# A retention and two feed-forward layers: the beginning and the first block join the played order

## The chip, the cores and the metric

The kernel runs on one core of one Trainium2 chip. The metric is the time of one execution on the device in microseconds (us). The engines are TensorE (PE, matmuls), VectorE (DVE), ScalarE (ACT), GpSimd (POOL) and SyncE (SP, which here issues nearly all transfers). Each engine takes its own instructions strictly in order.

## The reference

Three stages in float32, for 4 x 576 = 2304 tokens, 8 heads of 64, model width 512, inner width 2048:

```python
scores = q @ k.T / sqrt(64)                     # per batch and head
ret    = scores * where(i >= j, gamma_h ** (i - j), 0)
x      = (ret @ v), heads side by side          # 2304 x 512
h = x @ moe_w_in;   g = maximum(0.01 * h, h);  x = g @ moe_w_out
h = x @ moe2_w_in;  g = h * cos(h);            out = g @ moe2_w_out
```

## The kernel before

The tokens are cut into 18 chunks of 128 for the attention and into five blocks for the first layer (`TB`, line 27). The attention runs as a recurrence: per chunk `scores` (64 x 64 products of k and q), `masks` (DVE multiplies by the causal mask), `values` and `growth` (products with v, and the growth of the state), `states` (DVE adds the growth to the running state), `reads` (PE adds the state's share), and `take` (ACT scales the result into `xr`). `scale_q` and `scale_v` multiply a chunk's q and v by tables beforehand.

The first layer needs its operands as a high and a low half of 32 bits each, and the weights arrive as 64-bit words, two 32-bit words to a value. There are 16 weight tiles f (128 of the 2048 inner columns each; the tile holds its part of w_in and of w_out). One tile is converted by ACT (absolute value `conv_a` line 445, scaling of the low word line 446, cast to the high half line 473) and DVE (clamp 451, shift 453, sign 457, addition 464, and the low half, by subtraction, 476). Blocks of x are split likewise (`split_x`, ACT 492, DVE 493). `h_mm` (H, line 505) is x times a tile's w_in, `o_mm` (O, line 519) is g times its w_out: 12 matmuls each. Between them ACT applies the leaky ReLU and casts (530, 535), DVE makes g's low half (540). O trails H by two tiles (`LAG`): H0, H1, H2, O0, H3, O1 and so on. While a block runs, the chunks of the next are computed between its steps ("visits").

The order of work is written in two ways. The beginning (chunks 0 to 3) and block 0 are written out by hand in lines 1324 to 1434: transfers, attention and conversions in the order in which each engine is to take them. From block 1 on, `rest` gives every piece of work to a `Plan` (line 85) with an engine, an estimated duration, what it needs, and a due time; `play` (line 98) walks through it as a list scheduler would and writes the instructions in the order in which they began there. `dma` and `dve` add such tasks. The played part also converts the second layer's weights (lines 971 to 1043) beside blocks 1 to 3, and stores them for the second layer, which multiplies by Strassen-like sums.

SP waits for the landing of the eighth transfer before each new one, beside the buffers a transfer needs. A raw weight tile lies in the room of a later weight tile (`ROOM`, line 548), which it must leave before that tile is written.

Of the kernel before, what the change touches and what calls it, by code (L numbers as in the profile page):

```python
# [19 lines left out]
P = 128  # L20
# [6 lines left out]
TB = (512, 512, 512, 384, 384)  # L27
T0 = (0, 512, 1024, 1536, 1920)
# [24 lines left out]
G = 3  # L53
# [21 lines left out]

LATE, DRAIN = 12, 6
# [71 lines left out]
def retention_ffn_ffn(  # L148
# [43 lines left out]
    zero = xp.tile([P, 2 * T], F32, tag="x", name="zero")[:, :P]  # L192
# [23 lines left out]
    def scale_q(i):  # L216
        q = ch_t[i][:, 0]

        eng = nc.gpsimd if n_busy <= i < n_busy + 2 else nc.vector
        eng.tensor_tensor(out=q, in0=q, in1=itab_sb, op=ALU.mult)  # L220

    def scale_v(i):
        c = i % CYCLE * H
        if i in (1, 2) or n_first <= i < n_busy:
# [6 lines left out]
        eng = nc.gpsimd if 0 < i < n_busy + 2 else nc.vector  # L231
        eng.tensor_tensor(out=v3, in0=v3, in1=t3, op=ALU.mult)
# [86 lines left out]
    def growth(i):  # L319
# [16 lines left out]
        if i > n_first:  # L336
            last_of["rows"] = rows_done(got)
# [17 lines left out]
    def reads(i, part):  # L355

        v, ch = banks_of(i)[1], ch_t[i]
        behind = [last_of.pop("rows")] if part else []
# [19 lines left out]
        if not part:  # L378
            last_of["part", i] = last_of["rows"] = rows_done(last_of["pe", i])

    def both_reads(i):
        reads(i, 0)
        reads(i, 1)
# [11 lines left out]
    def take(i, ps=range(NP)):  # L395
# [39 lines left out]
    def words(g):
        r = raw_t[g].bitcast(U32).rearrange("p (x t) -> p x t", t=2)
        return r[:, :, 0], r[:, :, 1]

    def conv_a(g):
        lo, hi = words(g)  # L440
        n = lo.shape[1]
        whole = multi.tile([P, 2 * DM], F32, tag="t", name="t32")
        t = whole[:, :n]
        t_t[g], rawp_t[g] = t, whole
        nc.scalar.activation(t, hi.bitcast(F32), AF.Abs)
        nc.scalar.mul(lo.bitcast(I32), lo, 2.0**-29)

    def conv_b(g, between=lambda: None):
        lo, hi = words(g)
        t = t_t[g]  # L450
        nc.vector.tensor_scalar(t, t, W_LO, W_HI, op0=ALU.max, op1=ALU.min)
        u = t.bitcast(U32)
        nc.vector.tensor_scalar(  # L453
            u, u, 3, 0x3FFFFFF8, op0=ALU.logical_shift_left, op1=ALU.bitwise_and
        )
        between()
        nc.vector.scalar_tensor_tensor(  # L457
            out=u, in0=hi, scalar=0xC0000000, in1=u, op0=ALU.bitwise_and, op1=ALU.bitwise_or
        )

    def conv_c(g):
        lo, _ = words(g)
        i = t_t[g].bitcast(I32)
        nc.vector.tensor_tensor(out=i, in0=i, in1=lo.bitcast(I32), op=ALU.add)  # L464
        raw_t.pop(g)

    def w_part(g, half):
        l, f, s = g
        wt = w_t[l, f]
        return wt[:, half] if s is None else wt[:, half, s * DM : (s + 1) * DM]  # L470

    def conv_d(g):
        nc.scalar.copy(w_part(g, 0), t_t[g])

    def conv_e(g, eng):
        eng.tensor_tensor(
            out=w_part(g, 1), in0=t_t.pop(g), in1=w_part(g, 0).bitcast(F32), op=ALU.subtract
        )

    def new_w(l, f):  # L480
        w_t[l, f] = w_tile(f, [P, 2, 2 * DM], F32R, f"w{f}")


    x_t, h_t, g_t, graw = {}, {}, {}, {}

    def split_x(lj):
        n = TB[lj]
        for k in range(KK):
            x = xp.tile([P, 2, T], F32R, tag="x", name="x_sb")
            x_t[lj, k] = x  # L490
            raw = xr.pop((lj, k))[:, :n]
            nc.scalar.copy(x[:, 0, :n], raw)
            nc.vector.tensor_tensor(  # L493
                out=x[:, 1, :n], in0=raw, in1=x[:, 0, :n].bitcast(F32), op=ALU.subtract
            )
# [31 lines left out]
    def leaky(lj, f):  # L527
        hp = h_t.pop((lj, f))
        g = gp.tile([P, T], F32, tag="graw", name="graw", bufs=G)[:, : TB[lj]]
        nc.scalar.activation(g, hp, AF.Prelu, alpha=0.01)  # L530
        graw[lj, f] = g

    def g_high(lj, f):
        g_t[lj, f] = gp.tile([P, 2, T], F32R, tag="g", name="g")
        nc.scalar.copy(g_t[lj, f][:, 0, : TB[lj]], graw[lj, f])

    def g_low(lj, f):
        n = TB[lj]
# [54 lines left out]
    def rest():  # L593
# [53 lines left out]
        for s in range(NF, len(steps) + LAG):  # L647
# [841 lines left out]
```

## Time and profile before

| | us |
|---|---|
| three runs | 856.03, 856.01, 853.37 (median 856.01) |
| profiled execution | 853.42 |
| its span, first to last instruction | 851.3 |
| PE busy | 829.3 |
| DVE busy | 601.5 |
| ACT busy | 518.4 |
| POOL busy | 8.5 |

The mean granted clock of PE is 0.986 of full speed. The part of the execution outside the span is 2.1 us. Busy shares are means over stages: block 0 ends near 140 us, the first layer near 471, and the rest is the second layer.

### The profile page before, as it was taken

The numbers are of one execution on the slowest core, as the hardware profiler recorded it, in microseconds if no ns is written. First come the engines' busy times: TensorE is split into PE (matmuls) and PEld (weight loads), VectorE is DVE, ScalarE is ACT, GpSimd is POOL, SyncE is SP. The second block draws the span as 40 slices with busy tenths as digits, with TensorE's granted clock in tenths as the row PEclk, the third lists the DMA queues.
The fourth block names the chain that finished last, engine by engine and source line by source line (L and its number), as shares of the span: only waits on it lengthen the run. The fifth ranks groups of instructions, "written<-read, shape, count | busy, mean of one in ns | idle before, by whom it ended". The sixth has DMA issues, their size and how long they took to land.

```text
span 851.3 us, 16302 instructions
## 1 busy us (share of the span) xinstructions
PE 829.3 (97%) x6288; PEld 771.0 (91%) x6288; DVE 601.5 (71%) x1183; ACT 518.4 (61%) x1112; POOL 8.5 (1%) x9
## 2 busy tenths in 40 slices
PE   6699999999999999999999999999999999999998
PEld 6478888888888888999999999999999999999998
DVE  4799985776876757667511587889877876866762
ACT  4688864554655545555422688767678755677650
POOL 0000020000000000000000000000000000000000
PEclk7799999999999999999999999999999999999999
DMA  9925512656657866853790798798988697665312
GB/s 358 418 83 202 192 67 85 217 194 211 211 191 251 247 213 197 260 191 135 262 406 2 252 311 272 265 374 322 349 284 287 216 405 272 208 225 186 137 49 75
DMA packets 91949, 193.30 MB, mean 227 GB/s; under 512 B 7648, under 2 KB 55264, under 8 KB 81632
## 3 DMA queue, kind: packets, MB, share of 16 engines
q1 hardware_dynamic: 91728, 191.92, 64.2%
q8 instruction: 49, 0.80, 0.4%
q10 hardware_dynamic: 144, 0.35, 0.1%
q14 instruction: 28, 0.23, 0.1%
HBM read 143.22 MB, written 49.02 MB: 226 GB/s over the span
## 4 chain that ended last, share of the span: by engine, by line
PE 90%; DMA 4%; issue 3%; DVE 2%; ACT 1%; SPq 0%; POOLq 0%; DVEq 0%
PE psum L1239 23%; PE psum L519 22%; PE psum L505 21%; PE psum L1111 19%; DMA raw<-in_w 2%; PE psum L366 1%; PE psum L305 1%; PE psum L328 1%; PE psum L268 1%; DMA wa<-wa 1%; DMA ws<-ws 1%; DVE t L464 0%; DVE st L351 0%; DVE t L457 0%; DVE t L453 0%
## 5 line engine op out<-in xcount | busy, mean ns | idle before, releaser
L1239 PE MATMUL psum<-g,wo 128*128 128x384 f32 x1152 | 222.3, 334 | 0.0
L505 PE MATMUL psum<-x_sb,w 128*128 128x512 f32 (+1 forms) x960 | 214.2, 373 | 4.2 <-DVE x_sb L493 2.5
L519 PE MATMUL psum<-g,w 128*128 128x512 f32 (+1 forms) x960 | 212.0, 370 | 0.0
L505 PEld LDWEIGHTS psum<-x_sb,w 128*128 128x128 f32 x960 | 177.5, 190 | 29.7 <-DVE x_sb L493 2.7
L1239 PEld LDWEIGHTS psum<-g,wo 128*128 128x128 f32 x1152 | 201.7, 188 | 0.0
L519 PEld LDWEIGHTS psum<-g,w 128*128 128x128 f32 x960 | 174.3, 188 | 23.7
L1111 PE MATMUL psum<-x,ws 128*128 128x384 f32 x576 | 114.5, 335 | 1.3 <-ACT psum L1212 1.3
L1111 PEld LDWEIGHTS psum<-x,ws 128*128 128x128 f32 x576 | 100.9, 188 | 2.3 <-ACT psum L1212 1.9
L797 DVE TENSOR_TENSOR g<-graw,g 128x512 fp32r<-128x512 f32 (+1 forms) x64 | 39.9, 623 | 69.3 <-ACT g L794 69.0
L1111 PE MATMUL psum<-x,wa 128*128 128x384 f32 x432 | 86.1, 334 | 0.0
L1111 PEld LDWEIGHTS psum<-x,wa 128*128 128x128 f32 x432 | 75.9, 188 | 0.0
L1166 DVE SCALAR_TENSOR_TENSOR h<-r,h 128x384 f32<-128x384 f32 x96 | 52.9, 554 | 24.0 <-ACT r L1163 23.7
L794 ACT CAST g<-graw 128x512 fp32r<-128x512 f32 (+1 forms) x64 | 36.3, 568 | 48.8 <-PE psum L519 47.0
L790 ACT ACTIVATE graw<-psum 128x512 f32<-128x512 f32 (+1 forms) x64 | 34.7, 542 | 48.2 <-PE psum L505 47.5
L1162 ACT ACTIVATE r<-r 128x384 f32<-128x384 f32 x96 | 50.4, 525 | 21.2 <-DVE r L1155 20.7
L1150 DVE SCALAR_TENSOR_TENSOR r<-n,h 128x384 f32<-128x384 int32 x96 | 53.0, 552 | 11.9 <-ACT n L1147 11.5
L1176 DVE TENSOR_TENSOR g<-h,g 128x384 fp32r<-128x384 f32 x96 | 52.7, 553 | 10.9 <-ACT g L1173 10.3
L1147 ACT ACTIVATE n<-h 128x384 int32<-128x384 f32 x96 | 49.3, 519 | 8.4 <-DVE h L1139 8.0
L1155 DVE SCALAR_TENSOR_TENSOR r<-n,r 128x384 f32<-128x384 int32 x96 | 53.2, 554 | 1.6
L1173 ACT CAST g<-h 128x384 fp32r<-128x384 f32 x96 | 48.6, 509 | 7.6 <-DVE h L1166 7.3
L1163 ACT ACTIVATE r<-r 128x384 f32<-128x384 f32 x96 | 50.5, 526 | 2.0
L1258 DVE SCALAR_TENSOR_TENSOR acc<-psum,acc 128x384 f32<-128x384 f32 x48 | 26.7, 557 | 16.4 <-PE psum L1239 15.3
(81 smaller groups left out, 794.8 us busy)
## 6 DMA issues: line engine op xcount, KB each, us to landing
ws<-ws SPq DMA_DIRECT2D x24, 1024.0 KB, 7.1
wo<-wo SPq DMA_DIRECT2D x24, 1024.0 KB, 6.0
wa<-wa SPq DMA_DIRECT2D x24, 768.0 KB, 6.1
ch<-in_qkv SPq DMA_DIRECT2D x17, 1024.0 KB, 7.7
mraw<-in_w SPq DMA_DIRECT2D x64, 256.0 KB, 3.6
x<-xq SPq DMA_DIRECT2D x21, 768.0 KB, 9.6
raw<-in_w SPq DMA_DIRECT2D x15, 1024.0 KB, 9.1
xq<-m SPq DMA_DIRECT2D x84, 128.0 KB, 5.1
```

Source lines behind the costliest of these rows:

```text
L505: nc.tensor.matmul(hp, wt[:, i, cols], x_t[lj, k][:, j, :n], start=(k == 0 and a == 0), stop=(k == KK - 1 and a == 2),)
L519: nc.tensor.matmul(psum[:, BANK_O + m, :n], wt[:, i, cols], gt[:, j, :n], start=(f == 0 and a == 0), stop=(f == NF - 1 and a == 2),)
L1111: nc.tensor.matmul(bank[BANKS[m]], a[:, hl, i, j * P : (j + 1) * P], x[:, j, v, :], start=m in (1, 5) and j == 0 and n == 0, stop=j == 1 a ...
L1147: t = add("ACT", 515, lambda: nc.scalar.activation(n_ap(), hb.ap, AF.Copy, scale=INV_2PI), [t], due, 0, nb.old)
L1150: nc.vector.scalar_tensor_tensor(out=r_ap(), in0=n_ap(), scalar=-C1, in1=hb.ap, op0=ALU.mult, op1=ALU.add)
L1155: nc.vector.scalar_tensor_tensor(out=r_ap(), in0=n_ap(), scalar=-C2, in1=r_ap(), op0=ALU.mult, op1=ALU.add)
L1162: t = add("ACT", 515, lambda: nc.scalar.activation(r_ap(), r_ap(), AF.Sin, scale=0.5), [t], due)
L1163: t = add("ACT", 515, lambda: nc.scalar.activation(r_ap(), r_ap(), AF.Square), [t], due)
L1166: nc.vector.scalar_tensor_tensor(out=hb.ap, in0=r_ap(), scalar=0.5, in1=hb.ap, op0=ALU.subtract, op1=ALU.mult)
L1173: t = add("ACT", 515, lambda: nc.scalar.copy(gb.ap[:, 0], hb.ap), [t], due, 0, gb.old)
L1176: nc.vector.tensor_tensor(out=gb.ap[:, 1], in0=hb.ap, in1=gb.ap[:, 0].bitcast(F32), op=ALU.subtract)
L1239: nc.tensor.matmul(bank[m], wt[:, i, hl, m * P : (m + 1) * P], gt[:, v, :], start=h == 0 and z == 0 and x == 0, stop=h == 1 and z == 1 and ...
```

## The change

The hand-written beginning and block 0 go; both become tasks of the same plan. The helpers `load_raw`, `conv_a` to `conv_e`, `split_x`, `leaky`, `g_high`, `g_low` and the hand-written list are deleted; `first_chunk`, `first_weights` and `beginning` take their place. Plan time starts at `BEGIN` = 27 us for the first H. The instructions on a tile are the same, but tile 0, like tile 15 before, is converted in two halves of 512 columns (the w_in half, then the w_out half), and all tiles use two fixed buffers, f even the first, f odd the second. The widths of blocks 1 to 4 change order, so block 0 now has three chunks to visit for block 1 beside chunk 3's half visit, not four. POOL keeps only the scaling of chunk 3's v; the scalings of chunks 8 and 9, which it had, go to DVE.

```diff
-TB = (512, 512, 512, 384, 384)
-T0 = (0, 512, 1024, 1536, 1920)
+TB = (512, 384, 384, 512, 512)
+T0 = (0, 512, 896, 1280, 1792)
...
+BEGIN, IN_HALVES = 27, (0, NF - 1)
...
+    def v_by(i):
+        return {0: "DVE", 1: "ACT", 2: "ACT", 3: "POOL"}.get(i, "ACT" if i < n_busy else "DVE")
...
-        at, now = {}, 0.0
+        at, now = {}, BEGIN
...
+        def chunk(i, due):
+
+            old = () if i < n_first else read_of[i - n_first if i < n_first + 2 else i - 2]
+            t = dma(2650, lambda: load_chunk(i), old, due - 14, (), 4000 if i < n_first else 2500)
+            a = dve(DVE[512], lambda: scale_q(i), [t], due - 4)
...
+        def first_chunk(i):
+            due = i / 10 - SOON
+            if i:
+                chunk(i, 14 + i)
+            c = [add("PE", 900, lambda: scores(i), scaled[i], due)]
+            m = [add("DVE", 700, lambda: masks(i), c, due)]
+            v = [add("PE", 900, lambda: values(i), m, due)]
+            g = [add("PE", 900, lambda: growth(i), v, due)]
+            old = read_of.get(i - 1, ())
+            s_ = [add("DVE", 850, lambda: states(i), [*g, *read_of.get(("st", i - 1), ())], due, 0, old)]
+            read_of["st", i] = s_
+            a = add("PE", 500, lambda: reads(i, 0), s_, due)
+            mark = add("POOL", 60, lambda: None, [a], due)
+            read_of[i] = [add("PE", 500, lambda: reads(i, 1), [mark], due)]
+            taking(i, read_of[i], due)
...
+        def first_weights(f):
+
+            due = at["H", 0, f] - 9
+            halves = [slice(0, DM), slice(DM, 2 * DM)] if f in IN_HALVES else [slice(0, 2 * DM)]
+            tb, t32 = ((t0, t32_0), (t1, t32_1))[f % 2]
+            uses = [Use(b) for b in tb]
+            old_t = uses[0].old + uses[1].old
...
+            for n, h in enumerate(halves):
...
+                got = [loads[n]] if len(loads) > 1 else loads
+                d_ = due + n * 5
+                ab = add("ACT", 630 if one_ else 1140, lambda g=step: g("a"), got, d_, 0, old_t)
+                lo_ = add("ACT", 630 if one_ else 1140, lambda g=step: g("m"), got, d_)
+                t = dve(421 if one_ else 690, lambda g=step: g("c"), [ab], d_)
+                t = dve(421 if one_ else 690, lambda g=step: g("s"), [t], d_)
+                t = dve(690 if one_ else 1225, lambda g=step: g("o"), [t], d_)
+                t = dve(690 if one_ else 1225, lambda g=step: g("+"), [t, lo_], d_)
+                done_ += [t]
+                hi_ = add("ACT", 600 if one_ else 1050, lambda g=step: g("d"), [t], d_, 0, () if n else room_of.get(f, ()))
+                lw = dve(690 if one_ else 1225, lambda g=step: g("l"), [hi_], d_)
...
+        def beginning():
+            chunk(0, 0)
+            for i in range(n_first):
+                first_chunk(i)
+                if i >= 2:
+                    room_of[NF + 1 - i] = read_of[i]
+                room_of[NF // 2 - 1 - i] = read_of[i]
+            for f in range(NF):
+                first_weights(f)
+            split_block(0, 0)
...
-        load_chunk(0)
-        load_raw(0)
-        for i in range(1, n_first):
-            load_chunk(i)
-        for f in range(1, 4):
-            load_raw(f)
...
```

The transfers that SP issues first, before the change (`ch` is a chunk, `raw` a raw weight tile; raw_121 is tile 0, raw_129 tile 1):

```order
L211 DMA ch_118<-in_qkv 128x1024
L212 DMA ch_118<-in_qkv 128x1024
L427 DMA raw_121<-in_w 128x1024
L214 DMA ch_123<-in_qkv 128x2048
L214 DMA ch_125<-in_qkv 128x2048
L214 DMA ch_127<-in_qkv 128x2048
L427 DMA raw_129<-in_w 128x1024
L427 DMA raw_131<-in_w 128x1024
L427 DMA raw_133<-in_w 128x1024
```

And after it (raw_221 is tile 0, in two halves, raw_251 and raw_301 are tiles 1 and 2, raw_386 is tile 3):

```order
L213 DMA ch_151<-in_qkv 128x1024
L214 DMA ch_151<-in_qkv 128x1024
L216 DMA ch_154<-in_qkv 128x2048
L216 DMA ch_156<-in_qkv 128x2048
L216 DMA ch_176<-in_qkv 128x2048
L781 DMA raw_221<-in_w 128x512
L790 DMA raw_251<-in_w 128x1024
L790 DMA raw_301<-in_w 128x1024
L781 DMA raw_221<-in_w 128x512
L790 DMA raw_386<-in_w 128x1024
```

Tile 0 moves behind chunks 1 to 3, and its second half behind tiles 1 and 2.

DVE in the first chunks, before the change, from the scaling of chunk 2's q (ch_125) to the mask of chunk 3 (ch_127 is chunk 3, p_sb_334 and p_sb_373 are the masks of chunks 2 and 3, t32_171 is tile 0):

```order
L220 TENSOR_TENSOR ch_125<-ch_125,tabs_sb_109 128x512
L464 ISA t32_171<-raw_121,t32_171 128x2048
L220 TENSOR_TENSOR ch_127<-ch_127,tabs_sb_109 128x512
L288 TENSOR_TENSOR p_sb_334<-psum_112,tabs_sb_109 128x512
L476 TENSOR_TENSOR w0_315<-t32_171,w0_315 128x1024
L288 TENSOR_TENSOR p_sb_373<-psum_112,tabs_sb_109 128x512
```

After it, from the scaling of chunk 2's q (ch_156) to the mask of chunk 3 (ch_176 is chunk 3, p_sb_259, p_sb_326 and p_sb_365 are the masks of chunks 1, 2 and 3, st_321 and st_323 the states of chunk 1, mt_139 the buffer of tile 0):

```order
L221 TENSOR_TENSOR ch_156<-ch_156,tabs_sb_109 128x512
L292 TENSOR_TENSOR p_sb_259<-psum_115,tabs_sb_109 128x512
L221 TENSOR_TENSOR ch_176<-ch_176,tabs_sb_109 128x512
L355 TENSOR_TENSOR st_321<-psum_115,st_241 128x256
L355 TENSOR_TENSOR st_323<-psum_115,st_321 128x256
L292 TENSOR_TENSOR p_sb_326<-psum_115,tabs_sb_109 128x512
L827 TENSOR_SCALAR mt_139<-mt_139 128x512
L829 TENSOR_SCALAR mt_139<-mt_139 128x512
L292 TENSOR_TENSOR p_sb_365<-psum_115,tabs_sb_109 128x512
```

The scaling of chunk 3's q now stands ahead of chunk 1's states.

DVE between the last low half of x (x_sb_515) and the low half of tile 2 (w2_545), before the change:

```order
L493 TENSOR_TENSOR x_sb_515<-xr_295,x_sb_515 128x512
L476 TENSOR_TENSOR w1_518<-t32_336,w1_518 128x1024
L451 TENSOR_SCALAR t32_521<-t32_521 128x1024
L453 TENSOR_SCALAR t32_521<-t32_521 128x1024
L457 SCALAR_TENSOR_TENSOR t32_521<-raw_131,t32_521 128x1024
L464 ISA t32_521<-raw_131,t32_521 128x2048
L451 TENSOR_SCALAR t32_542<-t32_542 128x1024
L453 TENSOR_SCALAR t32_542<-t32_542 128x1024
L476 TENSOR_TENSOR w2_545<-t32_521,w2_545 128x1024
```

After it, the last twelve instructions up to the low half of tile 2 (w2_589; mt_140 holds tile 3 here, mt_139 first tile 0's second half and then tile 2, ch_522 is chunk 5):

```order
L841 TENSOR_TENSOR w0_444<-mt_139,w0_444 128x512
L829 TENSOR_SCALAR mt_140<-mt_140 128x1024
L833 SCALAR_TENSOR_TENSOR mt_140<-raw_386,mt_140 128x1024
L667 TENSOR_TENSOR g_150<-graw_147,g_150 128x512
L837 ISA mt_140<-raw_386,mt_140 128x2048
L827 TENSOR_SCALAR mt_139<-mt_139 128x1024
L829 TENSOR_SCALAR mt_139<-mt_139 128x1024
L833 SCALAR_TENSOR_TENSOR mt_139<-raw_301,mt_139 128x1024
L837 ISA mt_139<-raw_301,mt_139 128x2048
L841 TENSOR_TENSOR w3_584<-mt_140,w3_584 128x1024
L221 TENSOR_TENSOR ch_522<-ch_522,tabs_sb_109 128x512
L841 TENSOR_TENSOR w2_589<-mt_139,w2_589 128x1024
```

The conversion of tile 3 (w3_584) now ends ahead of that of tile 2, and the scalings of two chunks and two low halves of g stand ahead of it too. PE takes H0, H1, H2, O0, H3 in both kernels.

## Rows read from the trace of the kernel before

**Rows 1.** The page, parts 1 and 3: busy time by engine; queue of instructions.
```profile
PE 829.3 (97%) x6288; PEld 771.0 (91%) x6288; DVE 601.5 (71%) x1183; ACT 518.4 (61%) x1112; POOL 8.5 (1%) x9
...
q8 instruction: 49, 0.80, 0.4%
```

**Rows 2.** Stretches: length, busy us by engine (x instructions), clock, DMA share, GB/s.
```profile
18.98:44.41 25.43, 16.13 (x303) 12.35 (x296) 19.14 (x27) 17.27 (x32) 1.48 (x1) 0.75 1.01 417
48.67:140.13 91.46, 91.09 (x878) 74.47 (x876) 79.14 (x100) 66.62 (x124) 6.83 (x4) 1.00 0.31 107
140.13:402.26 262.13, 261.97 (x2293) 227.21 (x2294) 190.99 (x447) 144.21 (x335) 0.00 (x0) 1.00 0.64 210
...
471.21:504.00 32.79, 31.46 (x179) 30.45 (x178) 22.43 (x45) 24.94 (x54) 0.00 (x0) 1.00 0.92 296
```

**Rows 3.** PE in order of time: start us, us, work, idle time before and releaser.
```profile
21.42 0.40 PE L328 MATMUL psum<-ch 64*64 64x64 f32 x12
22.48 0.56 PE L328 MATMUL psum<-ch 64*64 64x64 f32 x20 [0.66 <-issue]
...
24.47 0.65 PE L305 MATMUL psum<-p_sb,ch 64*64 64x64 f32 x32
...
25.76 0.45 PE L366 MATMUL psum<-ch,st 64*64 64x64 f32 x12 [0.18 <-DVE st L351]
28.40 1.32 PE L366 MATMUL psum<-ch,st 64*64 64x64 f32 x20 [2.19 <-issue]
...
34.84 7.47 PE L505 MATMUL psum<-x_sb,w 128*128 128x512 f32 x24 [2.50 <-DVE x_sb L493]
...
44.46 4.37 PE L505 MATMUL psum<-x_sb,w 128*128 128x512 f32 x11 [0.76 <-DVE w L476]
...
54.77 1.94 PE L328 MATMUL psum<-ch 64*64 64x64 f32 x15 [0.34 <-ACT ch L227]
...
57.16 3.06 PE L519 MATMUL psum<-g,w 128*128 128x512 f32 x12
```

**Rows 4.** DVE in order of time, block 0.
```profile
60.38 0.69 DVE L451 TENSOR_SCALAR t<-t 128x1024 f32<-128x1024 f32 x1
...
65.24 0.68 DVE L288 TENSOR_TENSOR p_sb<-psum,tabs_sb 128x512 f32<-128x512 f32 x1
65.84 0.87 DVE L351 TENSOR_TENSOR st<-psum,st 128x256 f32<-128x256 f32 x2
66.63 0.68 DVE L540 TENSOR_TENSOR g<-graw,g 128x512 fp32r<-128x512 f32 x1
...
122.46 0.42 DVE L451 TENSOR_SCALAR t<-t 128x512 f32<-128x512 f32 x1
...
125.18 0.69 DVE L540 TENSOR_TENSOR g<-graw,g 128x512 fp32r<-128x512 f32 x1
```

**Rows 5.** ACT and DVE in order of time: first uses of landed tiles.
```profile
10.22 1.12 ACT L445 ACTIVATE t<-raw 128x1024 f32<-128x1024 f32 x1 [7.56 <-DMA raw<-in_w]
...
16.48 2.02 ACT L227 ACTIVATE ch<-ch,tabs_sb 128x64 f32<-128x64 f32 x8 [1.69 <-DMA ch<-in_qkv]
...
18.98 0.69 DVE L220 TENSOR_TENSOR ch<-ch,tabs_sb 128x512 f32<-128x512 f32 x1 [0.68 <-DMA ch<-in_qkv]
```

**Rows 6.** Stretches of 2 us at the start.
```profile
36.00:38.00 2.00, 2.00 (x7) 1.52 (x6) 2.00 (x3) 2.00 (x3) 0.00 (x0) 0.50 0.99 410
...
46.00:48.00 2.00, 2.00 (x6) 1.52 (x6) 1.97 (x3) 1.24 (x2) 0.00 (x0) 0.50 0.41 160
```

**Rows 7.** The chain that ended last, in order of time: start us, us, work.
```profile
129.22 2.72 PE psum L505 x12
...
140.13 8.64 PE psum L505 x36
...
328.58 4.24 PE psum L505 x24
```

More of the change, by code (lines that the diff above doesn't have):

```diff
@@ L357, in reads @@
         v, ch = banks_of(i)[1], ch_t[i]
-        behind = [last_of.pop("rows")] if part else []
+        behind = [last_of.pop(("rows", i))] if part else []
         for p in range(NP):
@@ L378, in reads @@
         if not part:
[L379 to L383, printed above, removed]
+            last_of["part", i] = last_of["rows", i] = rows_done(last_of["pe", i])
     def visit(i):
@@ L439, in conv_a @@
[L439 to L459, printed above, removed]
@@ L480, in new_w @@
[L480 to L495, printed above, removed]
+    w_t, raw_t = {}, {}
@@ L779, in ffn_h @@
                 needs = [pe, x_ready[j][x]]
-                if x == 0 and f != 1:
+                if not j:
+                    needs.append(w_in[f])
+                if x == 0 and f != 1 and k:
                     needs += h_read.get(k - 2 if f == 2 else k - 1, ())
@@ L825, in ffn_o @@
                 done["evac", j] = evacuations(j, ends)
-        first = chunks[2][0]
-        scaled = {i: [] for i in range(first, first + 2)}
-        read_of = {}
-        def chunk(i):
-            due = at["visit", i - 1]
-            if i not in scaled:
-                t = dma(2800, lambda: load_chunk(i), read_of[i - 2], due - 14)
-                a = dve(DVE[512], lambda: scale_q(i), [t], due - 4)
-                b = dve(DVE[512], lambda: scale_v(i), [t], due - 4)
-                scaled[i] = [a, b]
+        scaled, read_of = {}, {}
@@ new lines, in taking @@
+        def taking(i, needs, due):
+            j = max(j for j in range(NB) if T0[j] <= i * P)
+            old = x_ready.get(j - 1, ()) if i == chunks[j][0] else ()
+            t = needs
+            for p in range(NP):
+                t = [add("ACT", 380 if i % CYCLE != CROSS else 640, lambda p=p: take(i, (p,)), t, due, 0, old)]
+                taken[j, p] += t
+            read_of["take", i] = t
+            busy["early"] += t
+        def first_chunk(i):
[13 more added lines that the diff above has]
+            taking(i, read_of[i], due)
@@ L1348, in retention_ffn_ffn @@
-        scale_v(2)
-        states(0)
-        both_reads(0)
-        take(0)
-        scale_q(2)
-        scores(2)
-        add_of(0)
-        high_of(0)
-        scale_q(3)
-        scores(3)
-        masks(2)
-        ready(1)
-        scale_v(3)
-        values(2)
-        growth(2)
-        low_of(0)
-        masks(3)
-        states(1)
-        both_reads(1)
-        take(1)
-        values(3)
-        growth(3)
-        def second():
-            states(2)
-        conv_b(grains[1], second)
```

306 lines of the change are left out of this document (123 added, 183 removed).

## The prediction

> **What bounds the kernel now.** I read the page first, then stretches, then the start in order of time. On the page TensorE (PE) is busy 829.3 of 851.3 us [rows 1], so 22 us at most are to be had by ending waits. The stretches show where they lie: from 140.13 to 402.26 PE works 261.97 of 262.13 us, in block 0 from 48.67 on 91.09 of 91.46, and 31.46 of 32.79 where the second layer begins [rows 2]. What is left lies ahead of 48.67 or behind the last matmul, which the change does not touch. So I ask one thing: when does the unbroken run of PE begin, and how much work is behind it?
>
> In block 0 before, the first H tiles start at 34.84 and the matmuls of the third one (f=2) at 44.46, after which PE hardly stops [rows 3]. H(0,2) waits for its weight tile, which VectorE (DVE) converts. DVE is the second engine to watch: 79.14 of 91.46 us busy in block 0 [rows 2]. A whole tile costs it 4.86 us (five instructions, from the clamp at 60.38 to the mask at 65.24), a half tile 2.72 (122.46 to 125.18), a mask 0.60 (65.24 to 65.84), the low half of a g or an x the same (its busy time, 0.68, is the mask's), the states of a chunk 0.79 (65.84 to 66.63) [rows 4]. I take start-to-start times, since one instruction overlaps the next by about 0.09 us.
>
> **The change, part by part.**
>
> *Transfers.* Raw tile 0 goes behind chunks 1 to 3, and in halves. Before, it landed at 10.22, chunk 2 at 16.48 and chunk 3 at 18.98 [rows 5]. Chunk 3 takes chunk 2's place in the queue: 16.48, 2.50 earlier. The first half of raw tile 0 comes next, about 17.7 (half the 2.5 us of a whole one): 7.5 us later than before. The later tiles come every 2.5 us, and DVE needs 4.86 for each: the transfers themselves cost nothing from there on.
>
> *The first blocks on DVE.* On DVE the multiplication of chunk 3's q now stands ahead of chunk 1's states, and DVE takes its instructions in order. So what it has left at 16.48 is the states of chunks 1 to 3 and all that stands ahead of the low half of w2. The order there is also new: w3 is finished before w2, because tile 0's second half holds the buffer that w2 shares with it. PE still takes H(0,2) third, with O(0,0) behind it, so H(0,2) waits for both tiles. Sum from 16.48 until w2 is whole:
> w1, w3 and w2 whole, 3 x 4.86 = 14.58; w0 in halves, 2 x 2.72 = 5.44; four low halves of x, two of g, the scaling of q for chunks 3, 4 and 5, nine x 0.60 = 5.40 (a scaling is busy for 0.69, rows 5); masks of chunks 2 and 3, 1.20; three states, 2.37. Together 29.0 us. Before, DVE did 19.14 us of work between chunk 3's landing and 44.41, and stood idle for 6.29 [rows 2]. So the change puts 9.9 us more work in front of H(0,2), of which 2.50 are paid by the earlier chunk.
>
> Lower end: 16.48 + 29.0 = 45.5, without a wait on DVE. Upper end: the idle time of before on top, 51.8. I take 3.5 us of waits, from following the order: mask 3 for its scores 0.5, states 2 for their products 0.5, w1's clamp for ScalarE (ACT) 0.4, g(0,0)'s low half for PE and two ACT instructions 0.7, w3's clamp behind them 0.3, and 1.1 for the stall below. That gives 49.0, against 44.46 before: 4.5 us later, with ends 1.0 and 7.3.
>
> *The stall "issue".* Before, PE stood for 2.19 us at 26.2 in the reads of chunk 2, waiting for nothing that the profile shows, and 0.66 at 21.8 in a growth [rows 3]. Between the two lie 20 + 16 + 16 + 32 + 32 + 12 = 128 passes, each a load and a matmul, 256 instructions; the instruction queue moved 49 packets for 12,576 of PE's [rows 1], 257 each. So I read it as a wait for the program's own code behind the weight transfers, and it hangs on the count of instructions, not on the time. In the new order the same count (476 passes from the start) again falls on the 12th pass of chunk 2's reads, with the queue as full as before. I therefore leave it in, shortened by the slower approach.
>
> *H(0,0) and H(0,1).* From chunk 3's landing to H(0,0) before: 15.86 us. The chain is the same, with a conversion of half the size within it, so about 14, and PE starts at 30.5 rather than 34.84, 4 us earlier. This gains nothing: both finish near 38, and PE waits about 10 us for w2.
>
> *TensorE's clock.* After the pause ahead of 34.84 it ran at half (0.50 until 38, rows 6), and 24 matmuls took 7.47 us where full speed needs 24 x 0.227 = 5.45 (2.72 per 12, rows 7): 2.0 lost. Before, H(0,2) also lost it: after PE's pause ahead of 44.46 the clock was 0.50 in 46 to 48, and 11 matmuls took 4.37 for 2.50, 1.9 lost [rows 3, 6]. After a pause of 10 us I expect the same loss of 2.0: 0.1 more. The Trainium skill ("TensorE: Matmul & The Clock Gate", Part 1: The HAM clock gate) says that idling drops the array to 1.2 GHz and steady work brings it back; the trace agrees. By that rule a start brought forward and then left waiting pays the slow clock twice, and by the rule's opposite H(0,2) would cost 2.0 less, a sum of 0.6 rather than 2.6.
>
> *Given back.* Before, H(0,3) ended at 54.43 (0.34 ahead of 54.77) and O(0,1) began at 57.16 [rows 3]: 2.73 us for 24 small matmuls that waited for ACT's scaling of chunk 4 and then ran at its pace. Now this scaling stands ahead of H(0,2), during PE's pause, and their 48 passes need 1.0 at the rate of others (32 in 0.65, rows 3): 1.7 gained. The step from block 0 to block 1 goes from 512 wide to 384: before, three H's took 8.64 there, 0.48 over 3 x 2.72, where the step to a 384 block took 4.24 for two, 0.08 over [rows 7]: 0.3 gained after what follows them.
>
> *Work moved from GpSimd (POOL) to DVE* (q and v of chunks 7 to 9), one chunk's visit fewer in block 0: DVE's count up to the last tile changes by under 1 us. It is then some 3 us ahead of where it was at the same tile, since w3 and two scalings are done; after H(0,4), whose tile w4 comes only just in time, PE does not wait for it. If that cover were gone, H(0,4) would be up to 1.2 us (one low half) late.
>
> *Widths.* All blocks hold the same matmuls in another order: two of 384 and three of 512. Cost 0, with 1.3 gained at best where the second layer begins, if the longer last block gives ACT more room (PE idle there: 32.79 - 31.46, rows 2).
>
> **The sum**: 4.5 + 0.1 - 1.7 - 0.3 = +2.6 us. The profiled execution took 853.42, so 856.0 on its own level. The three runs are 856.03, 856.01 and 853.37; the profile belongs to the lower level, the median to the upper, 2.6 apart, and nothing in the profile tells which the changed kernel will show. I add 1.0, less than half: 857.0.
>
> **Rivals.**
>
> *The waits on DVE vanish.* For it: ACT is busy 17.27 of 25.43 us in that stretch [rows 2], so its part can be ready ahead of DVE's. Then H(0,2) runs at 45.5: 1.0 + 0.1 - 1.7 - 0.3, and the 1.3 at the second layer, -2.2: 851.2, faster. Against it: DVE has 29 us of work behind one landing, so this is a floor, and all six waits counted above would have to go.
>
> *The second layer's conversion gets too tight.* It runs from the second block to the last, 262.13 us with DVE busy 190.99, 73% [rows 2]. One of its three blocks turns narrow: 16 pairs of steps at 4.24 for 5.44 [rows 7], 19.2 us less, and one visit more (128 passes, at most 2.6): 245.5 us, in which DVE gets some 5 us more (POOL's scalings, the visit): 196, 80%. If low halves of g come late by 0.15 in each of 32 narrow steps, 4.8 more: 861.8. It decides where what stands ahead of a low half on DVE exceeds a narrow pair of steps, 4.24 us. Against it: in block 0 DVE is 87% busy and PE loses 0.37.
>
> *Nothing moves.* Both kernels begin their unbroken run when DVE has brought w2, and what is lost is returned in full at O(0,1) and the block steps: within 1 us, 854.0 to 856. For it: the two are bound by the same engine.
>
> **Chances.** H(0,2) late as worked out, 0.45: +1 to +4.5. Waits vanish, 0.22. Too tight, or more waits at the start than I count, 0.20. Nothing moves, 0.13. A difference of 0.3% (2.6 us) is about what a measurement of this kernel can tell. The first case lies half within it and half above; the second is mostly faster; the third slower; the fourth none: faster 0.20, same 0.40, slower 0.40. Range: floor 851.2, upper 853.42 + 7.3 + 0.1 - 2.0 = 858.8 and the upper level or the third case beyond it: 851 to 862. The likeliest case alone: 854.4 to 859.
>
> **What would show it.** Chunk 3's scaling on DVE at 16.5; H(0,0) near 30.5; a gap of about 10 us on PE ahead of H(0,2), ended by DVE's low half of w2, with w3's just before it; an "issue" stall at the 12th pass of chunk 2's reads; a clock of 0.50 under H(0,2); O(0,1) near 60. I am wrong if w2 is whole before 46, if PE stops elsewhere in block 0, or if PE idles within the 384 blocks.

## The result, and the profile after

| | before | after |
|---|---|---|
| median | 856.01 us (853.3 to 856.26, 5 runs) | 860.13 us (859.46 to 861.54, 5 runs) |
| ratio, 95% interval | | 1.0062 (1.0042 to 1.0083) |
| profiled execution, its span | 853.42, 851.3 | 861.54, 859.6 |

The change makes the kernel slower by 4.1 us, 0.6%. Predicted were 857.0 (851 to 862). The two profiled executions lie further apart, 8.1: that of before is of the kernel's lower level, that of after the slowest of its five. So the traces tell where the time goes; the size is the medians' to tell, which lie about half as far apart.

The first lines of the page after: the sums have hardly changed, PE is busy 829.1 us as before [rows 1]. The loss is all waiting.

```profile
PE 829.1 (96%) x6288; PEld 771.1 (90%) x6288; DVE 603.8 (70%) x1193; ACT 518.9 (60%) x1107; POOL 1.7 (0%) x5
...
q8 instruction: 49, 0.80, 0.4%
```

PE in order of time, after (columns as in [rows 3]); L309 is `values`, L370 `reads`, L433 H, L447 O:

```profile
19.02 0.41 PE L309 MATMUL psum<-p_sb,ch 64*64 64x64 f32 x13
22.06 0.80 PE L309 MATMUL psum<-p_sb,ch 64*64 64x64 f32 x18 [2.63 <-issue]
...
25.12 0.40 PE L370 MATMUL psum<-ch,st 64*64 64x64 f32 x3
...
25.22 0.62 PE L370 MATMUL psum<-ch,st 64*64 64x64 f32 x10
28.26 1.30 PE L370 MATMUL psum<-ch,st 64*64 64x64 f32 x19 [2.42 <-issue]
...
34.51 7.45 PE L433 MATMUL psum<-x_sb,w 128*128 128x512 f32 x24 [2.33 <-DVE x_sb L603]
51.40 0.79 PE L433 MATMUL psum<-x_sb,w 128*128 128x512 f32 x1 [9.44 <-ACT w L839]
53.20 5.06 PE L433 MATMUL psum<-x_sb,w 128*128 128x512 f32 x11 [1.00 <-DVE w L841]
...
61.06 2.95 PE L433 MATMUL psum<-x_sb,w 128*128 128x512 f32 x12
...
65.01 3.05 PE L447 MATMUL psum<-g,w 128*128 128x512 f32 x12
```

The second stall stands behind the 3 and 10 passes, the 13th of chunk 2's reads. H(0,0) starts when it did before (34.51, 34.84), H(0,2) 8.74 us later than before (53.20, 44.46; here and below by its last eleven matmuls, where nothing else is said), and O(0,1) 7.85 later (65.01, 57.16). From there on the kernels nearly keep their distance: the spans end 8.3 apart.

DVE in order of time, after: the landing of chunk 3, the waits longer than 0.3 us, and the low halves of w3 and w2 (L841):

```profile
16.43 0.69 DVE L221 TENSOR_TENSOR ch<-ch,tabs_sb 128x512 f32<-128x512 f32 x1 [2.34 <-DMA ch<-in_qkv]
...
23.69 0.95 DVE L355 TENSOR_TENSOR st<-psum,st 128x256 f32<-128x256 f32 x2 [2.28 <-PE psum L332]
...
29.61 0.95 DVE L355 TENSOR_TENSOR st<-psum,st 128x256 f32<-128x256 f32 x2 [3.16 <-PE psum L370]
...
40.48 0.69 DVE L667 TENSOR_TENSOR g<-graw,g 128x512 fp32r<-128x512 f32 x1 [1.27 <-ACT g L664]
41.52 0.69 DVE L827 TENSOR_SCALAR mt<-mt 128x1024 f32<-128x1024 f32 x1 [0.34 <-ACT mt L823]
...
50.18 1.22 DVE L841 TENSOR_TENSOR w<-mt,w 128x1024 fp32r<-128x1024 f32 x1
...
51.92 1.22 DVE L841 TENSOR_TENSOR w<-mt,w 128x1024 fp32r<-128x1024 f32 x1
```

Two waits stand out: the states of chunks 2 and 3, 2.28 and 3.16 us, each right behind one of PE's stalls "issue". The stretches of after (columns as in [rows 2]) show DVE's work between the landing of chunk 3 and a whole w2, that block 0 loses nothing behind H(0,2) and the blocks up to 400 us only 0.29, and that H(0,2) ran at the lower of the clock's two levels, 1.2 GHz, as in [rows 6]:

```profile
16.43:53.14 36.71, 17.05 (x316) 13.38 (x311) 28.85 (x43) 26.62 (x49) 1.48 (x1) 0.64 0.86 346
53.20:145.00 91.80, 91.80 (x776) 75.78 (x777) 82.14 (x113) 62.60 (x105) 0.00 (x0) 0.97 0.29 104
145.00:400.00 255.00, 254.71 (x2454) 232.57 (x2453) 177.05 (x410) 137.72 (x322) 0.00 (x0) 1.00 0.63 205
...
54.00:56.00 2.00, 2.00 (x6) 1.52 (x6) 1.93 (x3) 2.00 (x5) 0.00 (x0) 0.50 0.00 0
```

### The profile page after: what moved, and what is told of

Read it like the earlier page. It is cut to its first block, busy times and chain, and to the rows that moved or that the text cites. A ratio compares the mean times of both kernels' runs of the same rounds, so it can differ in the third digit from the quotient of the medians.

```text
span 859.6 us, 16278 instructions
## 1 busy us (share of the span) xinstructions
PE 829.1 (96%) x6288; PEld 771.1 (90%) x6288; DVE 603.8 (70%) x1193; ACT 518.9 (60%) x1107; POOL 1.7 (0%) x5
## 4 chain that ended last, share of the span: by engine, by line
PE 90%; DMA 4%; issue 3%; DVE 2%; ACT 1%; SPq 0%; DVEq 0%; POOLq 0%; ACTq 0%
PE psum L1261 23%; PE psum L447 22%; PE psum L433 22%; PE psum L1133 19%; DMA ch<-in_qkv 2%; PE psum L309 1%; PE psum L370 1%; PE psum L332 1%; DMA xq<-m 1%; PE psum L272 1%; DMA ws<-ws 1%; DMA y<-graw 1%; DVE mt L833 0%; DVE mt L837 0%; DVE w L841 0%
## 5 line engine op out<-in xcount | busy, mean ns | idle before, releaser
L433 PE MATMUL psum<-x_sb,w 128*128 128x512 f32 (+1 forms) x960 | 215.6, 375 | 12.8 <-ACT w L839 9.4
L447 PE MATMUL psum<-g,w 128*128 128x512 f32 (+1 forms) x960 | 212.6, 371 | 0.1
L433 PEld LDWEIGHTS psum<-x_sb,w 128*128 128x128 f32 x960 | 177.9, 191 | 38.5 <-ACT w L839 9.9
L447 PEld LDWEIGHTS psum<-g,w 128*128 128x128 f32 x960 | 174.7, 188 | 24.3 <-DVE graw L624 0.5
L667 DVE TENSOR_TENSOR g<-graw,g 128x512 fp32r<-128x512 f32 (+1 forms) x80 | 50.9, 637 | 71.0 <-ACT g L664 70.4
L664 ACT CAST g<-graw 128x512 fp32r<-128x512 f32 (+1 forms) x80 | 46.3, 579 | 62.8 <-PE psum L447 58.8
L660 ACT ACTIVATE graw<-psum 128x512 f32<-128x512 f32 (+1 forms) x80 | 44.3, 554 | 65.2 <-PE psum L433 62.8
L1280 DVE SCALAR_TENSOR_TENSOR acc<-psum,acc 128x384 f32<-128x384 f32 x48 | 26.7, 557 | 16.3 <-PE psum L1261 15.3
```

Source lines behind the costliest of these rows:

```text
L433: nc.tensor.matmul(hp, wt[:, i, cols], x_t[lj, k][:, j, :n], start=(k == 0 and a == 0), stop=(k == KK - 1 and a == 2),)
L447: nc.tensor.matmul(psum[:, BANK_O + m, :n], wt[:, i, cols], gt[:, j, :n], start=(f == 0 and a == 0), stop=(f == NF - 1 and a == 2),)
L667: nc.vector.tensor_tensor(out=g.ap[:, 1, :n], in0=y.ap[:, :n], in1=g.ap[:, 0, :n].bitcast(F32), op=ALU.subtract)
```

## The experiments

Theory: the loss is the time at which DVE has brought w2, made later by its order (w3 first, tile 0 in halves) and by stalls of PE that come from program code waiting behind weight transfers. Rivals: the block widths; DVE's plain amount of work. Times of before differ a little from one set of runs to the next, so each result is given with its ratio to the runs of before in its own set, and the 95% interval of that ratio. Where the intervals of two kernels overlap, their times alone show no difference, and what is said rests on the traces.

### Widths, and DVE's order

**Widths as before.**

```
-TB = (512, 384, 384, 512, 512)
+TB = (512, 512, 512, 384, 384)      (T0 to match)
```

> The changed kernel with the widths of the blocks as before (512, 512, 512, 384, 384). Theory (the loss lies ahead of H(0,2)): within 1 us of the changed kernel, 859 to 861, with the same wait of about 9.4 us. Rival (two narrow blocks make the second layer's conversion tight): the time falls by some 3 to 5 us to 855 to 857, and idle time of PE between 140 and 400 us goes.

861.10 us, 1.0070 (1.0054 to 1.0087), and the same wait of 9.44 ahead of H(0,2). The widths play no part that these runs can tell; the rival "too tight" falls, which wanted a shorter time here.

**Tile 0 whole.**

```
-BEGIN, IN_HALVES = 27, (0, NF - 1)
+BEGIN, IN_HALVES = 27, (NF - 1,)
```

> The changed kernel with tile 0 converted whole again (one transfer, one set of instructions). Theory (the loss is the 9.4 us wait ahead of H(0,2) for w2, and w2 is late because tile 0's second half holds its buffer, so that w3 and a scaling go ahead of it on DVE): DVE then finishes w2 ahead of w3 and without 4.86 + 0.60 + 0.58 us of the work that stood ahead of it, so H(0,2) starts near 47 rather than 53.2, PE's wait there falls from 9.4 to about 4 us, and the time falls by about 6 us to 854. Rival (widths, or second-layer conversion that is too tight): no change, 860. Rival (only the two stalls named issue cost the time): no change either, since they stay.

858.34, 1.0036 (1.0022 to 1.0050). PE in order of time, this kernel:

```profile
47.51 0.50 PE L433 MATMUL psum<-x_sb,w 128*128 128x512 f32 x1 [3.38 <-ACT w L839]
48.77 4.23 PE L433 MATMUL psum<-x_sb,w 128*128 128x512 f32 x11 [0.76 <-DVE w L841]
...
83.22 2.80 PE L433 MATMUL psum<-x_sb,w 128*128 128x512 f32 x11 [1.18 <-DVE w L841]
```

The wait falls to 3.38, as expected, but the eleven matmuls of H(0,2) come 4.4 us earlier than after, not 6 (the expectation set the first matmul, 47.51, against 53.20, the first of the eleven). O(0,1) begins at 59.71, 5.3 earlier, and the spans are 3.5 apart (856.1, 859.6); the median gains 1.8, less than that, since the profiled execution of after is the slowest of its five. A new wait of 1.18 stands at 83.22: PE is now far enough ahead that it waits for DVE once more in block 0.

**w2 ahead of w3**, by other conversion buffers:

```
-            tb, t32 = ((t0, t32_0), (t1, t32_1))[f % 2]
+            tb, t32 = ((t0, t32_0), (t1, t32_1))[f % 2 if f < 2 else (f + 1) % 2]
```

> The changed kernel with w2 in tile 1's buffer and w3 in tile 0's (the later tiles alternate accordingly), so that w2 is finished ahead of w3, with tile 0 still in halves. Theory: w2 takes w3's place on DVE, low half done at 51.4 rather than 53.1, H(0,2) 1.8 us earlier, 858.3; less than without the halves, because the four first steps of both tiles are still done before either low half. Rival (the halves alone, not the order of the two tiles, hold H(0,2)): no change, 860.

858.80, 1.0044 (1.0029 to 1.0060). PE, this kernel:

```profile
51.34 4.53 PE L433 MATMUL psum<-x_sb,w 128*128 128x512 f32 x11 [1.48 <-DVE w L841]
```

H(0,2) comes 1.9 earlier (51.34, 53.20), the 1.8 expected. The median is 1.3 lower, but the interval overlaps that of after (1.0042 to 1.0083).

**O(0,0) ahead of H(0,2)**, in PE's pause:

```
-            slots += old + new if s and s % NF == 0 else new + old
+            slots += old + new if s and (s % NF == 0 or s == LAG) else new + old
```

> The changed kernel with O(0,0) ahead of H(0,2) in PE's order. Theory (PE waits there for DVE alone, and what O(0,0) needs, the low half of g(0,0) at 41.2 and w0's second half at 42.8, is there early): O(0,0) runs within the wait, H(0,2) still starts with w2 near 53, and what follows comes 2.7 to 3 us earlier: 857. It may gain up to 1 us more from a clock that stays up. Rival (w2's conversion waits for PE, over g or a buffer): H(0,2) moves back by O(0,0)'s length and the time stays at 860.

858.93, 1.0046 (1.0028 to 1.0063). PE in order of time, this kernel (L447 is O):

```profile
43.98 2.82 PE L447 MATMUL psum<-g,w 128*128 128x512 f32 x11 [0.32 <-DVE w L841]
52.51 0.80 PE L433 MATMUL psum<-x_sb,w 128*128 128x512 f32 x1 [5.71 <-ACT w L839]
```

O(0,0) runs within the pause, the wait ahead of H(0,2) shrinks from 9.44 to 5.71, and the profiled span by 2.2 (857.4, 859.6). H(0,2) itself comes 1.1 later (54.30), and the median is 1.2 lower, less than the 3 expected and with overlapping intervals.

### The stalls "issue"

**Fewer warming matmuls.** If the stall hangs on a count of instructions, work taken from the front moves it back in the program.

```
-WARM = (16, 2)
+WARM = (8, 2)
```

> The kernel after with 8 instead of 16 warming matmuls at the start, 16 passes fewer ahead of everything. Theory (the stall hangs on the count of instructions): both stalls come 16 passes later in the program, at about the 29th pass of chunk 2's values instead of the 13th, and at about the 28th of chunk 2's reads instead of the 12th, and PE goes on at the same times, 22.1 and 28.3 us, when the code has come. Rival (the stall belongs to the work at that place, such as chunk 2's values and reads): the same 13th and 12th pass. H(0,0) 34.5 in both; time 860 in both.

860.86 in one run. PE in order of time:

```profile
19.09 0.64 PE L309 MATMUL psum<-p_sb,ch 64*64 64x64 f32 x29
22.12 0.27 PE L309 MATMUL psum<-p_sb,ch 64*64 64x64 f32 x2 [2.38 <-issue]
...
24.51 0.45 PE L370 MATMUL psum<-ch,st 64*64 64x64 f32 x13 [0.16 <-POOLq L259]
28.31 0.48 PE L370 MATMUL psum<-ch,st 64*64 64x64 f32 x3 [3.36 <-issue]
```

The first stall moved from behind the 13th pass of the values to behind the 29th, 16 on; the second to behind the 13 of the reads' second sixteen, 29 in all, from 13. PE goes on at the same times, 22.1 and 28.3. So the stall hangs on the count, and its end on something that comes at a set time. The instruction queue's 49 packets for 0.80 MB [rows 1] are 16.3 KB each. The Trainium skill ("Trainium Architecture — The Big Picture", The software stack) gives an instruction 64 bytes, so 256 of them 16 KB: the trace agrees. The same section has the instruction streams brought into the engines' memory when the program is loaded; the packets of this trace move while it runs, and the measurement decides.

**Later raw tiles, by the planner's needs.**

```
-                    loads.append(dma(2650, load, room_of.get(ROOM[f], ()), due - 14, ...
+                    loads.append(dma(2650, load, [*room_of.get(ROOM[f], ()), *(read_of[n_first - 1] if f > 1 else ())], due - 14, ...
```

> Raw tiles 2 and later wait for the reads of chunk 3, so the transfer queues are not full while PE needs the program code of chunks 2 and 3. Theory (PE's code comes behind the weight transfers): the second stall called issue, 2.42 us ahead of 28.26 in the kernel after, falls under 1; the first, 2.63 ahead of 22.06, stays mostly, since chunk 4 and tile 1 still fill the queues there; H(0,0) near 32 instead of 34.51; H(0,2), whose tile w2 is now also converted ahead of w3, near 48; median 857 to 858. Rival (a stall that belongs to each 256 instructions, whatever the queues carry): both stalls as before, H(0,0) at 34.5, H(0,2) near 50, median 859.

862.10, 1.0082 (1.0064 to 1.0100): a miss, and by my own edit. A need of the planner sets only SP's order; no semaphore holds the transfer back. Tile 15 and raw tiles 2 and later followed chunk 5 at once, and the DMA share stayed at 0.92 to 1.05 from 20 to 36 us. The second stall grew to 4.06 us, the packet came at 27.5. With a later packet PE went on later, which speaks for the theory by the other sign.

**The same, with tile 0 whole** (both edits above):

> Tile 0 whole again (as in the run with whole tiles) and raw tiles 2 and later behind the reads of chunk 3. Theory: H(0,0) near 32.5, H(0,2) near 45.5 instead of 47.51, but DVE is then the bound of block 0, so PE waits again at a later H and only part of it stays: median 856 to 858. Rival (DVE has room later in block 0): the whole 3.4 us of H(0,2) is kept against the run with whole tiles, median 855.

859.63, 1.0053 (1.0035 to 1.0072), second stall 2.69, the first matmul of H(0,2) at 49.14: the queues were as full here, so the expectation had no ground.

**The kernel before with raw tiles 2 and 3 behind chunks 4 and 5.** There the order on SP does hold them back, since chunk 5 waits for chunk 1's reads. Raw tile 4 moves behind chunk 5 with them.

```
-        for f in range(1, 4):
-            load_raw(f)
+        load_raw(1)
...
         load_chunk(4)
-        load_raw(4)
         load_chunk(5)
-        for f in range(5, 10):
+        for f in range(2, 10):
```

> The kernel before with raw tiles 2 and 3 issued behind chunks 4 and 5 (which wait for the first chunks' buffers) instead of at the start, and nothing else moved. Theory (code behind weight transfers): the stall of 2.19 us ahead of 28.40 falls under 1, H(0,0) from 34.84 to below 33, H(0,2) from 44.46 to 42 or 43, median 853 to 854. Rival (the stall is not from the transfers): 2.2 us as before, H(0,0) at 34.8, median 855 as before, or later if tiles 2 and 3 now come too late.

851.80, 0.9962 (0.9948 to 0.9977): faster than before. Two stretches of this kernel (columns as in [rows 2]; the last three are the clock, the DMA share and GB/s), and PE in order of time:

```profile
23.00:24.00 1.00, 0.46 (x16) 0.32 (x16) 0.99 (x2) 0.06 (x1) 0.00 (x0) 1.00 0.01 0
41.64:44.31 2.67, 2.67 (x11) 2.19 (x12) 2.64 (x3) 2.20 (x2) 0.00 (x0) 1.00 1.02 420
```
```profile
25.64 0.46 PE L366 MATMUL psum<-ch,st 64*64 64x64 f32 x16 [0.18 <-DVE st L351]
26.25 0.46 PE L366 MATMUL psum<-ch,st 64*64 64x64 f32 x16 [0.15 <-POOLq L255]
...
31.35 8.13 PE L505 MATMUL psum<-x_sb,w 128*128 128x512 f32 x24 [2.49 <-DVE x_sb L493]
40.38 0.50 PE L505 MATMUL psum<-x_sb,w 128*128 128x512 f32 x1 [0.91 <-ACT w L473]
41.64 2.83 PE L505 MATMUL psum<-x_sb,w 128*128 128x512 f32 x11 [0.76 <-DVE w L476]
...
51.95 2.03 PE L328 MATMUL psum<-ch 64*64 64x64 f32 x15 [1.91 <-ACT ch L227]
...
54.87 3.95 PE L519 MATMUL psum<-g,w 128*128 128x512 f32 x12
```

The queues run empty at 23, the packet has come by then, and the reads that stood for 2.19 us in [rows 3] run through. H(0,0) is 3.5 earlier, H(0,2) 2.8, O(0,1) 2.3 (54.87, 57.16). O(0,1) then took 3.95 us for 3.06, at a granted clock of 0.50 in 54 to 56 us, and the profiled spans end only 0.9 apart (850.4, 851.3). The medians are 4.0 apart; the profiled execution of before lies 2.6 under its median, so the traces give the smaller figure.

**After with empty queues.** Raw tile 2 takes the room of chunk 2, so that it must wait for its reads. Raw tiles 3 and later, the halves of tile 15 and chunks 4 and 5 are issued behind it; of the edit only the first line is shown.

```
-    ROOM = (13, 12, 11, 10, 9, 8, 15, 14, ...)
+    ROOM = (13, 12, 15, 10, 9, 8, 11, 14, ...)
...
```

> The kernel after with the queues really empty: raw tile 2 takes the room of chunk 2, so it has to wait for chunk 2's reads, and raw tiles 3 and later and chunks 4 and 5 are issued behind it. Theory (code behind transfers, and the stalls are what DVE's waits were mis-sized by): no stall of 2.4 us in chunk 2's reads, the first (2.63) shorter than 2.2; H(0,0) 32 instead of 34.51; DVE's waits for the states of chunks 2 and 3 together under 3.2 instead of 5.44; H(0,2) near 49 (2.4 from the stall, 1.8 because w2 is now converted beside w3 and done first); median 856 to 857.5. Rival (the amount of DVE's work alone sets H(0,2)): only the 1.8 of the order, H(0,2) at 51.3, median 858.8.

859.10, 1.0047 (1.0029 to 1.0064). PE in order of time:

```profile
21.82 0.79 PE L309 MATMUL psum<-p_sb,ch 64*64 64x64 f32 x18 [2.51 <-issue]
...
25.83 1.30 PE L370 MATMUL psum<-ch,st 64*64 64x64 f32 x19 [0.22 <-issue]
...
32.09 8.02 PE L433 MATMUL psum<-x_sb,w 128*128 128x512 f32 x24 [2.33 <-DVE x_sb L603]
...
49.65 4.79 PE L433 MATMUL psum<-x_sb,w 128*128 128x512 f32 x11 [1.54 <-DVE w L845]
...
78.22 2.79 PE L433 MATMUL psum<-x_sb,w 128*128 128x512 f32 x11 [0.69 <-DVE w L845]
...
103.34 2.79 PE L433 MATMUL psum<-x_sb,w 128*128 128x512 f32 x11 [0.81 <-DVE w L845]
```

DVE's waits for the states of chunks 2 and 3:

```profile
23.45 0.95 DVE L355 TENSOR_TENSOR st<-psum,st 128x256 f32<-128x256 f32 x2 [2.16 <-PE psum L332]
...
27.18 0.95 DVE L355 TENSOR_TENSOR st<-psum,st 128x256 f32<-128x256 f32 x2 [0.97 <-PE psum L370]
```

The second stall fell from 2.42 to 0.22, H(0,0) came to 32.09, DVE's waits for the two states fell from 5.44 to 3.13, and H(0,2) to 49.65: the theory's numbers, but for the first stall, which stayed (2.51; its packet came at 19.0). The median is nearer the rival's, since later waits give much of it back: 0.69 and 0.81 above, and smaller ones, together 2.6 of the 4.0 that O(0,1) had won.

**Empty queues and tile 0 whole** (both edits):

> Tile 0 whole and the queues empty while the code of chunks 2 and 3 comes. Theory: H(0,2) at 45 instead of 47.51 in the run with whole tiles; but DVE then bounds block 0 and PE waits longer than 1.18 us ahead of a later H, so that 0.5 to 1.5 of the 2.5 remain: median 857. Rival: all of it is kept, median 855.8.

855.39, 1.0010 (0.9997 to 1.0023): as fast as before. The median is the rival's, though the theory's longer wait at a later H is there too. More was won than expected: the first matmul of H(0,2) comes at 42.57, not 45. PE in order of time:

```profile
30.54 8.29 PE L433 MATMUL psum<-x_sb,w 128*128 128x512 f32 x24 [2.52 <-DVE x_sb L603]
42.57 0.80 PE L433 MATMUL psum<-x_sb,w 128*128 128x512 f32 x1 [3.74 <-ACT w L843]
44.81 4.75 PE L433 MATMUL psum<-x_sb,w 128*128 128x512 f32 x11 [1.44 <-DVE w L845]
...
56.13 3.07 PE L447 MATMUL psum<-g,w 128*128 128x512 f32 x12
...
80.66 2.79 PE L433 MATMUL psum<-x_sb,w 128*128 128x512 f32 x11 [2.40 <-DVE w L845]
```

The account closes: O(0,1) 8.88 earlier than after (56.13, 65.01), 2.40 lost again at 80.66, leaves 6.48; the spans are 6.5 apart (853.1, 859.6). This does not make the change free: the kernel before gains from empty queues too, and with them it runs at 0.9962 (851.80), 0.5% ahead of this one; H(0,2) stands at 41.64 there and at 44.81 here.

The packets of the instruction queue were found in half-microsecond windows of the DMA view. One of them, the half microsecond from 19.5 in the kernel after (queue: packets, MB, share of 16 engines):

```profile
q1 hardware_dynamic: 30, 0.18, 85.6%
q8 instruction: 1, 0.02, 13.4%
```

The packets against PE's stalls:

| kernel | packet in the half us from | PE goes on at | stall |
|---|---|---|---|
| before | 19.5; 26.0 | 22.48; 28.40 | 0.66; 2.19 |
| after | 19.5; 25.5 | 22.06; 28.26 | 2.63; 2.42 |
| later tiles, full queues | 19.5; 27.5 | 22.12; 29.96 | 2.72; 4.06 |
| the same, tile 0 whole | 18.5; 25.0 | 21.43; 27.90 | 1.26; 2.69 |
| after, empty queues | 19.0; 23.0 | 21.82; 25.83 | 2.51; 0.22 |
| the same, tile 0 whole | 18.5; 22.0 | 21.19; no stall | 0.27; 0 |
| before, late tiles 2 and 3 | 19.0; 22.5 | no stall | 0; 0 |

Wherever PE stood, it went on 2.4 to 3.0 us behind the start of the half microsecond with its packet.

### Chunk 4's scaling

**One step earlier, in the kernel before with late tiles.**

```
-            if s + 1 in visits and visits[s + 1] + 1 < n_busy:
-                scale_q(visits[s + 1] + 1)
-                scale_v(visits[s + 1] + 1)
+            ahead = 2 if s == 1 else 1
+            if s + ahead in visits and visits[s + ahead] + 1 < n_busy and s != 2:
+                scale_q(visits[s + ahead] + 1)
+                scale_v(visits[s + ahead] + 1)
```

> The kernel before with late tiles 2 and 3, and the scaling of chunk 4's q and v one step earlier, behind H(0,1) instead of H(0,2). This is the one part of the change that I had priced as a gain, 1.7 us. Theory: the wait of 1.91 us ahead of the visit at 51.95 goes, its 48 small matmuls run at full rate, O(0,1) begins near 52.3 instead of 54.87, tile w4 is up to 1.3 later, which H(0,4) does not feel; median 849.5 to 850.5 against 851.8. Rival (DVE bounds block 0, 17.79 of 18 us busy): the gain is given back at a later H of block 0, median 851.8.

849.75, 0.9939 (0.9922 to 0.9955): the lowest median, some 10 us ahead of the changed kernel. PE in order of time:

```profile
49.12 3.06 PE L505 MATMUL psum<-x_sb,w 128*128 128x512 f32 x12 [1.38 <-ACT graw L530]
...
53.20 3.04 PE L519 MATMUL psum<-g,w 128*128 128x512 f32 x12
```

O(0,1) comes 1.67 earlier (54.87 to 53.20), less than expected, since a wait of 1.38 for ACT's reading of H(0,2) is new. O(0,1) also takes 3.04 us for 3.95: the clock granted in 54 to 56 us is 1.00 here and was 0.50 without this edit. The profiled spans are 3.0 apart (847.4, 850.4); DVE does not take it back.

**ACT's part behind that reading.**

```
             leaky(0, s)
+            if s == 2:
+                scale_q(n_first)
+                scale_v(n_first)
```

> The run with chunk 4's scaling one step earlier, with ACT's part now behind the reading of H(0,2)'s products instead of ahead of it; there, H(0,3) had to wait 1.38 us for that reading. Theory (block 0 of this kernel is bound by PE's waits at its beginning, not by DVE): the 1.38 go, the visit of chunk 4 still finds its chunk scaled, and the whole amount stays: median 848.4 against 849.75. Rival (DVE, 17.79 of 18 us busy there, takes over): H(0,4) or a later one waits instead, median 849.7.

850.62, 0.9942 (0.9921 to 0.9962): no different. The wait ahead of H(0,3) is gone but for 0.22, and no later H waits for DVE, so neither account holds. In the profiled run H(0,0) came 1.05 later (32.70), O(0,1) at 53.05 all the same; what was lost lies behind it, such as 1.2 us of idle PE between 200 and 400 us for 0.2. That profiled execution is also the slowest of its six. What makes these differences stays open.

## Why the prediction was right, and where it was wrong

The direction, the place and the mechanism were right: PE's unbroken run begins when DVE has brought w2, later than before. The size was not, and that the time lies in the stated range is in part luck: the likeliest case alone ended at 859, under the 860.13 measured, and the range reached 862 only for the upper level and for the case of a tight second layer or more waits at the start than counted. Of that case the first half did not happen and the second did. Each step, in the profiled runs:

| step | predicted | measured |
|---|---|---|
| chunk 3 lands | 16.48 | 16.43 |
| DVE's work until w2 is whole | 29.0 | 28.9 busy; 29.7 is all but the four waits |
| its waits in between | 3.5 (0 to 6.3) | 7.7 (7.05 of it the four shown) |
| H(0,2) against before | +4.5 | +8.74 |
| the clock under it | +0.1 | +0.69 (5.06 for 4.37) |
| given back at O(0,1), as what is left | -1.7 | -1.58 |
| the rest of the kernel | -0.3 | +0.45 |
| sum | +2.6 | +8.3 (medians: +4.1) |
| H(0,0) | 30.5 | 34.51 |
| pause ahead of H(0,2) | about 10 | 9.44 |
| O(0,1) | near 60 | 65.01 |

**The term that was mis-sized**: "I take 3.5 us of waits, from following the order". They are 53.14 - 16.43 - 29.0 = 7.7, outside my upper end by 1.4. I had priced the stall at 1.1 in DVE's account and left the first one, 0.66 before, out of it. What I had written down held: the stall hangs on the count of instructions, and the second falls on the 12th or 13th pass of chunk 2's reads. But I did not draw the consequence. If the code comes at a set time, an earlier chunk only makes PE wait longer for it: PE stood from 19.4 on instead of from 21.8, and the first stall grew from 0.66 to 2.63. "Shortened by the slower approach" was the wrong sign. Both stalls now fall where DVE has nothing else to do, on the states of chunks 2 and 3. With the packet brought forward by 2.5 us these two waits fell by 2.3 and H(0,0) came to 32.09, so this cause is shown. My upper end was DVE's idle time of before, in which only one of the stalls stands.

The waits are what the forecast missed, not most of the loss. Against before, w2 is whole 8.7 us later (53.14, 44.41): 9.9 of more work ahead of it, 2.55 less by the earlier chunk (16.43, 18.98), and 1.4 of more waiting (7.7, 6.29). So the order of DVE's work, as forecast, makes the larger part, and the run with tile 0 whole, which takes some of it away, moves H(0,2) by 4.4.

**H(0,0) at 30.5** failed by the same step: the reads of chunks 2 and 3 end with the code, not with the chunks. I was saved by what I had said of it, that it gains nothing. The pause of 9.44 came out by luck: it began at 41.96 rather than near 38, and ended about as much later.

**The clock**: after its pause of 9.44 us PE ran at 1.2 GHz (granted 0.50) in 54 to 58 us, and in 34 to 38 too, so the slow level was paid twice, as it had been before [rows 6]. This agrees with the rule I had weighed (the Trainium skill, "TensorE: Matmul & The Clock Gate", Part 1: The HAM clock gate). I missed that nearly all of the eleven matmuls would be slow: 5.06 us for 4.37, 0.6 more than I had counted.

**The rivals**: "waits vanish" did not happen. "Too tight" is excluded by PE's 254.71 of 255.00 us between 145 and 400 and by the run with the old widths. Something like it shows in block 0 when H(0,2) comes earlier: PE waits there for DVE's low halves of later tiles, at 78 to 103 us (1.18, 0.69 and 0.81, 2.40). "Nothing moves" is excluded by the interval.

**Given back**, 1.7, was right: between the end of H(0,3) and O(0,1) lie 1.00 us (64.01 to 65.01), as forecast, for 2.73 before. The 1.67 of the run that moves chunk 4's scaling alone comes about otherwise, from a wait of 1.91 that ends and one of 1.38 that is new.

**Open**: why the medians differ by 4.1 where the profiled runs differ by 8.1. The profiled execution of before lies 2.6 under its median and that of after 1.4 above, which makes up the 4.0; no run here tells what makes one kernel's times differ so.

## What to carry to other kernels

In these kernels the wait called "issue", at a fixed count of instructions under full transfer queues, was a wait for program code. Look for the packet of the instruction queue ahead of its end. It ended at a set time, so work brought forward ahead of it only waited longer. Price it as a time of arrival, not as a length, and gain on it by issuing transfers that are not yet needed behind something that really waits. An earlier start can be lost again later to an engine that is nearly always busy: with the new order of DVE's work 1.2 to 2.6 us were given back in its waits, with the old order nothing. So read the later waits before counting a gain as whole.

## What the runs showed of the hardware

- PE's code arrived while the program ran, in packets of 16.3 KB, about 257 instructions each (49 for 12,576), by the same 16 DMA engines as the data (13.4% beside 85.6% in the half microsecond shown). Under full queues, at some 420 GB/s, they came 5.5 to 8 us apart; where the queues ran empty and PE was waiting or close to it, 3.5 to 4.5.
- A pause of the same length did not cost the same clock. Ahead of H(0,2) PE waited 0.91 us and then 0.76 in the kernel before with late tiles, and its eleven matmuls took 2.83 us, at a granted clock of 1.00; in the kernel before the waits were 0.89 and the same 0.76, and they took 4.37, at a granted clock of 0.50 in 46 to 48 us [rows 3, 6]. What decides between the two stays open.
